# RetNet recurrence with RWKV channel mix: order of the first loads, scaling per 256 tokens, mixes in halves, one function table

## The chip, the cores and the metric

The kernel runs on one core of a Trainium2 chip. The metric is device time in microseconds (us), from launch to end. The numbers of before are the median, the lowest and the highest of three runs, and one profiled execution beside them, whose trace all the lines below come from. Its engines are TensorE (PE, with its weight loads as PEld), VectorE (DVE), ScalarE (ACT), GpSimd (POOL) and SyncE (SP).

## The reference

Two layers follow each other. The first is a retention layer: for each batch (4) and head (8) a 64x64 state decays by a factor per head and takes in k times v at each of 768 tokens; q times the state is the output. The second is a channel mix: each token is mixed with the one before it by two vectors, then goes through two products with a squared ReLU between them, and through a sigmoid gate.

```python
def _attn_ref(q, k, v):
    ...
    for t in range(S):
        state = gamma[None, :, None, None] * state + np.einsum('bhd,bhe->bhde', k[:, :, t], v[:, :, t])
        y[:, :, t] = scale * np.einsum('bhd,bhde->bhe', q[:, :, t], state)
    return y

def _moe_ref(x, mu_k, mu_r, w_k, w_v, w_r):
    x_prev = ...                      # x, one token later; zero at the first
    xk = mu_k * x + (1.0 - mu_k) * x_prev
    xr = mu_r * x + (1.0 - mu_r) * x_prev
    k = np.maximum(xk @ w_k, 0.0)
    v = k * k @ w_v
    r = 1.0 / (1.0 + np.exp(-(xr @ w_r)))
    return r * v
```

x is the first layer's output with its 8 heads side by side (512 wide); the hidden width is 1024. q, k, v, the weights and the output are float32 in memory.

## The kernel before

**Tiling.** The 4 x 768 tokens are cut into 24 chunks of 128 tokens; two chunks make a block of 256, of which there are 12 (three to a batch). The first layer works chunk by chunk. Inside a chunk the recurrence is a masked product of q and k (`scores`, `masked`) times v, and between chunks a 64x64 state for each head is carried (`state`, `kept`). The second layer works block by block.

**One chunk of the first layer.** `load_q` and `load_v` bring 256 KB each through GpSimd's DMA queue, cast to float16; `load_k` brings k as float32 through SyncE's. `scale_k` (L169) multiplies k by the decay of each token and casts it (`ks`): on VectorE in the first two blocks, on GpSimd after them. `transposes` (L177) turns q and ks on TensorE, `transposed` (L181) copies the result out on ScalarE (`qkT`). `scores` (L188) multiplies, `masked` (L196) applies the mask on VectorE (`a2t`). `state` (L208, L216) and `kept` (L225, `sbd`) carry the state. `result` (L236, L242) makes the output in PSUM, and `decayed` (L252) writes it, times a table of decay powers `gy`, into `xT`, where a batch stands with its channels on the partitions.

**One block of the second layer.** `differ` (L266) takes xT minus xT one token earlier (`dx`): on VectorE in the first two blocks, on GpSimd after them. `mixed` (L272) makes `xk` and `xr` from it, four instructions each on VectorE, each with two float32 inputs in SBUF (`dx` and `xT`). `keys` (L282) is the product with w_k in four groups, `squared` (L292, L293) does ReLU and square on ScalarE; `gate` (L298) and `opened` (L305) do the product with w_r and the sigmoid for two halves of 128 tokens; `values` (L313) is the product with w_v, two parts for each half; `store` (L322) multiplies both on VectorE and sends the result through SyncE's queue.

**What sets the order.** Nothing is scheduled by a planner at build time. Each step is put into one list by `at` with a time, the list is sorted, and the steps are emitted in that order; each engine and each DMA queue then runs its own instructions in the order of emission and waits for what they need. The times come from the table `ORDER`, in units in which a block has T = 12: `att` has the offsets of the first layer's steps for the first and second chunk of a block (`scale`, `T` and `TC` for transposing and copying, `S` and `SE` for the state, `A`, `M`, `Y`, `YE` for scores, mask, result and output), and of `dx`, `xk` and `xr`; `mix` has those of the second layer (`G` keys, `K` squares, `R` and `RS` gate, `V` values, `O` store); `load` those of the loads of q and v from chunk 6 on; `start` the places of the first four blocks. From block 4 on the first layer runs two blocks ahead of the second.

**The start.** At time -9T come the loads: k of chunks 0 and 1 on SyncE with the constants between them, then on GpSimd q and v of chunks 0 to 3, both halves of w_k, q and v of chunks 4 and 5, w_r and both halves of w_v. k has two buffers of one chunk (`ldk`), so that k of chunk c + 2 is fetched when chunk c has been scaled (L341). `constants` (L374) also makes `gy` on VectorE: a copy and seven doublings for each of the two chunk parities, 14 multiplies (L386).

Of the kernel before, what the change touches and what calls it, by code (L numbers as in the profile page):

```python
# [9 lines left out]
F16 = mybir.dt.float16  # L10
F32 = mybir.dt.float32
# [38 lines left out]
def kernel(  # L50
# [40 lines left out]
    g0_np = 0.125 * KSC * np.stack([gam[h_pj] ** -C, one], axis=1)  # L91
# [10 lines left out]
    ld = pool("ld", 8)  # L102
# [49 lines left out]
    def load_k(c):  # L152
        b, t = tok(c)
        K32[c] = ldk.tile([P, H, D], F32, name="k32")
        nc.sync.dma_start(out=K32[c], in_=k[b, :, t, :].rearrange("h t d -> t h d"))

    def load_q(c):
        b, t = tok(c)
        Q16[c] = ld.tile([P, H, D], F16, name="q16")
        nc.gpsimd.dma_start(out=Q16[c], in_=q[b, :, t, :].rearrange("h t d -> t h d"))  # L160

    def load_v(c):
        b, t = tok(c)
        V16[c] = ld.tile([P, H, D], F16, name="v16")
        nc.gpsimd.dma_start(out=V16[c], in_=v[b, :, t, :].rearrange("h t d -> t h d"))  # L165

    def scale_k(c, eng):
        KS[c] = att.tile([P, H, D], F16, name="ks16")
        eng.tensor_tensor(  # L169
            out=KS[c], in0=K32[c], in1=gk[:, c % 2, :, None].to_broadcast([P, H, D]), op=ALU.mult  # L170
        )

    def transposes(c):
        PT[c] = psa.tile([P, 2, NJ, C], F16, name="pT", tag="a")
        for i, src in enumerate((Q16[c], KS[c])):
            for j in range(NJ):
                nc.tensor.transpose(PT[c][:, i, j, :], src[:, 2 * j : 2 * j + 2, :], ident)  # L177
# [284 lines left out]
```

## Time and profile before

| | |
|---|---|
| median of three runs | 189.29 us (188.75 to 189.69) |
| the profiled execution | 187.1 us |
| its span, first to last instruction | 185.3 us |
| granted TensorE clock | 0.999 |
| busy share: PE, DVE, ACT, POOL | 85%, 81%, 51%, 48% |
| matmuls | 1416 |
| DMA packets | 82336, of which 76560 under 512 bytes |
| HBM read, written | 24.22 MB, 6.29 MB |

The span is what the instructions take; the rest of the profiled execution's time lies before the first and after the last of them. Busy shares are means over the whole span. A matmul's duration includes the time in the pipeline, so that chained matmuls overlap; the chain of waits gives the time from one to the next. In the rows, a line such as L272 is a line of the kernel; `x4` is a count; a row of the timeline has start, duration, engine, line and tile, and in brackets the idle time before it and what ended it. A row of a line's own view has least, median and longest duration in ns. The row of a DMA issue has its size at the destination and the time from issue to landing. Where busy time by stage is shown, the last three columns are the granted clock, the DMA engines' share and GB/s.

### The profile page before, as it was taken

Reading aid. Unit: us, or ns where it says so; the run is one execution under the profiler, and the core shown is the slowest. Engines: PE = TensorE matmul, PEld = TensorE weight load, DVE = VectorE, ACT = ScalarE, POOL = GpSimd, SP = SyncE. Lnnn points to the kernel's source line nnn. Section 1 sums busy time; section 2 is a strip of 40 time slices with the busy share of each in tenths; the row PEclk is TensorE's granted clock in tenths of the full one; section 3 lists DMA queues with packets and bytes.
Section 4 is the critical chain, followed back from the end, with each engine's and each line's share of the span. In section 5 each row is a group of like instructions: output and inputs, shape, how many; then the busy total and the mean of one; then the engine's idle time right before and its main releaser. Section 6 shows DMA issues by size and latency. Waiting matters only on the chain.

```text
span 185.3 us, 3522 instructions
## 1 busy us (share of the span) xinstructions
PE 156.7 (85%) x1416; PEld 101.5 (55%) x1416; DVE 149.7 (81%) x237; ACT 94.3 (51%) x146; POOL 88.1 (48%) x87
## 2 busy tenths in 40 slices
PE   0374069899699999999899899899799899999991
PEld 0253047774375675558358468467367367475740
DVE  0845599995939798899999989999999989795511
ACT  2120121999374475508808709709519529557650
POOL 7993120407995793938809709619528021040000
PEclk9999999999999999999999999999999999999999
DMA  6999999920999899797993994995984111011112
GB/s 89 166 167 192 177 178 195 179 47 0 118 187 196 192 170 135 94 144 167 130 152 74 141 128 80 142 161 56 181 125 31 58 57 60 2 57 57 60 57 113
DMA packets 82336, 21.83 MB, mean 118 GB/s; under 512 B 76560, under 2 KB 79248, under 8 KB 82320
## 3 DMA queue, kind: packets, MB, share of 16 engines
q0 software_dynamic: 52560, 8.92, 61.5%
q1 hardware_dynamic: 28704, 12.69, 28.4%
q8 instruction: 11, 0.18, 0.4%
q10 hardware_dynamic: 1056, 0.00, 0.3%
q14 instruction: 5, 0.04, 0.1%
HBM read 24.22 MB, written 6.29 MB: 165 GB/s over the span
## 4 chain that ended last, share of the span: by engine, by line
PE 45%; DVE 37%; DMA 10%; ACT 2%; POOL 2%; issue 1%; SPq 1%; DVEq 0%
PE pV L313 15%; PE pZ L282 15%; DVE xr L272 14%; DVE xk L272 12%; DMA k<-in_k_dram 10%; PE pY L242 4%; PE pR L298 4%; DVE osb L322 3%; PE pA L188 3%; DVE a2t L196 3%; PE pY L236 3%; DVE sbd L225 2%; POOL dx L266 2%; DVE xT L252 2%; ACT k L293 1%
## 5 line engine op out<-in xcount | busy, mean ns | idle before, releaser
L292 ACT ACTIVATE kr<-pZ 128x512 f32<-128x512 f32 x48 | 28.4, 592 | 47.8 <-PE pZ L282 47.8
L282 PE MATMUL pZ<-xk,wk 128*128 128x256 f16 x384 | 47.8, 274 | 2.3 <-DVE xk L272 2.3
L313 PE MATMUL pV<-wv,k 128*128 128x512 f16 x192 | 49.0, 380 | 0.2 <-DVE osb L322 0.2
L266 POOL TENSOR_TENSOR dx<-xT 128x1024 f32<-128x1024 f32 x10 | 19.2, 1918 | 60.0 <-DVE xT L252 60.0
L272 DVE SCALAR_TENSOR_TENSOR xr<-dx,mur,xT 128x256 f16<-128x256 f32 x48 | 42.5, 944 | 0.0
L282 PEld LDWEIGHTS <-wk 128*128 128x128 f16 x384 | 36.4, 98 | 9.3 <-issue 3.0
L181 ACT COPY qkT<-pT 128x1024 f16<-128x1024 f16 x24 | 24.1, 1005 | 27.2 <-PE pT L177 27.0
L196 DVE TENSOR_TENSOR a2t<-pA,c_sb 128x512 f16<-128x512 f32 x48 | 30.1, 678 | 2.5 <-PE pA L188 2.5
L272 DVE SCALAR_TENSOR_TENSOR xk<-dx,muk,xT 128x256 f16<-128x256 f32 x48 | 28.8, 657 | 2.9 <-POOL dx L266 2.8
L293 ACT ACTIVATE k<-kr 128x512 f16<-128x512 f32 x48 | 30.2, 630 | 1.6
L169 POOL TENSOR_TENSOR ks<-k,csm_sb 128x512 f16<-128x512 f32 x20 | 22.8, 1143 | 12.1 <-DVE sbd L225 7.8
L313 PEld LDWEIGHTS <-k 128*128 128x128 f16 x192 | 16.9, 98 | 17.5 <-issue 0.8
L322 DVE SCALAR_TENSOR_TENSOR osb<-pV,rsb 128x512 f32<-128x512 f32 x24 | 16.4, 682 | 10.6 <-PE pV L313 7.3
L298 PE MATMUL pR<-wr,xr 128*128 128x512 f16 x96 | 24.1, 380 | 0.0
L160 POOL DMA_DIRECT2D q<-in_q_dram x24 | 22.2, 924 | 0.8 <-POOLq L446 0.8
L165 POOL DMA_DIRECT2D v<-in_v_dram x24 | 21.9, 914 | 0.0
L252 DVE TENSOR_TENSOR xT<-pY,gy_sb 128x512 f32<-128x512 f32 x24 | 16.5, 688 | 3.0 <-PE pY L242 2.8
L305 ACT ACTIVATE rsb<-pR 128x512 f32<-128x512 f32 x24 | 14.1, 590 | 6.5 <-PE pR L298 6.5
L177 PE MATMUL pT<-c_sb,q 128*128 128x128 f16 x96 | 10.2, 234 | 7.6 <-DMA q<-in_q_dram 7.6
L225 DVE TENSOR_TENSOR sbd<-pS,csm_sb 128x512 f16<-128x512 f32 x20 | 13.6, 681 | 3.1 <-PE pS L216 3.1
L298 PEld LDWEIGHTS <-xr 128*128 128x128 f16 x96 | 8.7, 98 | 10.0 <-DVE xr L272 0.6
L177 PEld LDWEIGHTS <-q 128*128 128x128 f16 x96 | 7.5, 104 | 10.3 <-DMA q<-in_q_dram 7.9
(26 smaller groups left out, 101.9 us busy)
## 6 DMA issues: line engine op xcount, KB each, us to landing
k<-in_k_dram SPq DMA_DIRECT2D x24, 256.0 KB, 5.4
out_dram<-osb SPq DMA_DIRECT2D x24, 256.0 KB, 2.3
q<-in_q_dram POOLq DMA_DIRECT2D x24, 128.0 KB, 4.8
v<-in_v_dram POOLq DMA_DIRECT2D x24, 128.0 KB, 5.8
wk<-in_moe_w_k_dram POOLq DMA_DIRECT2D x2, 512.0 KB, 12.1
wv<-in_moe_w_v_dram POOLq DMA_DIRECT2D x2, 512.0 KB, 18.5
wr<-in_moe_w_r_dram POOLq DMA_DIRECT2D x1, 512.0 KB, 17.5
c_sb<-c SPq DMA_DIRECT2D x1, 64.0 KB, 3.6
```

Source lines behind the costliest of these rows:

```text
L160: nc.gpsimd.dma_start(out=Q16[c], in_=q[b, :, t, :].rearrange("h t d -> t h d"))
L169: eng.tensor_tensor(out=KS[c], in0=K32[c], in1=gk[:, c % 2, :, None].to_broadcast([P, H, D]), op=ALU.mult)
L181: nc.scalar.copy(out=QKT[c], in_=PT.pop(c))
L196: nc.vector.tensor_tensor(out=A2[c][:, hp], in0=PA[c][hp], in1=causal[:, None, :].to_broadcast([P, NJ, C]), op=ALU.mult,)
L266: eng.tensor_tensor(out=DX[m], in0=xcur, in1=xprev, op=ALU.subtract)
L272: nc.vector.scalar_tensor_tensor(out=dst[m][:, j], in0=DX[m][:, j], scalar=mu[:, j : j + 1], in1=xprev[:, j], op0=ALU.mult, op1=ALU.add,)
L282: nc.tensor.matmul(pZ[:, i, :], lhsT=wk16[:, co, fo * P : fo * P + P], rhs=XK[m][:, co, :], start=(i == 0 and co == 0), stop=(co == NCO - ...
L292: nc.scalar.activation(out=kr, in_=PZ.pop((m, g)), func=AF.Relu)
L293: nc.scalar.activation(out=K2[m][:, 2 * g : 2 * g + 2], in_=kr, func=AF.Square)
L298: nc.tensor.matmul(pR, lhsT=XR[m][:, co, tb * P : tb * P + P], rhs=wr16[:, co, :], start=(co == 0), stop=(co == NCO - 1),)
L313: nc.tensor.matmul(PV[m, tb], lhsT=K2[m][:, fo, tb * P : tb * P + P], rhs=wv16[:, fo, :], start=(fo == 0), stop=(fo == NFO - 1),)
L322: nc.vector.scalar_tensor_tensor(out=osb, in0=PV.pop((m, tb)), scalar=1.0 / (KSC * KSC), in1=RS.pop((m, tb)), op0=ALU.mult, op1=ALU.mult,)
```

## The change

Six things, all in the order and the size of steps; what is computed stays the same.

1. **First loads.** k of chunks 0 to 3 is fetched through GpSimd's queue, and the queue's order becomes q, k, v of chunk 0, then of chunk 1, 2 and 3, then w_k as before. From chunk 4 on k stays on SyncE.
2. **Loads per 256 tokens.** The tiles of q, k and v hold a block. Each is filled by two DMAs of the same size as before, issued one after the other. k has two buffers of a block; the fetch of block n + 2 follows the scaling of block n. From block 3 on q and v have a place of their own in the order (`load`).
3. **Scaling per 256 tokens.** On GpSimd one instruction scales a block. In the first two blocks VectorE still scales chunk by chunk (`first`).
4. **Mixes in halves.** `mixed` does two of its four instructions at a time, each half with an offset of its own.
5. **Decay powers.** Only the even parity is built by doublings (`powers`); the odd one is one multiply from it (`powers2`). Both have a place of their own in the order.
6. **Function table.** A sigmoid of one column is run in `constants`, ahead of all other work of ScalarE.

All offsets of `ORDER` are new. The diff, cut where lines only follow from these:

```diff
     "att": {
-        "scale": (-5.73, -4.03),
-        "T": (0.1, 2.32),
-        "TC": (2.23, 4.28),
-        "S": (1.83, 6.57),
-        "SE": (2.9, 11.39),
-        "A": (2.81, 7.79),
-        "M": (6.42, 8.52),
-        "Y": (8.93, 10.34),
-        "YE": (9.06, 10.4),
-        "dx": (13.61,),
-        "xk": (14.87,),
-        "xr": (24.22,),
+        "scale": (-7.68,),
+        "first": (-5.03, 0.72),
+        "T": (-0.46, 2.67),
+        "TC": (-0.22, 2.89),
+        "S": (2.03, 6.44),
+        "SE": (5.18, 12.2),
+        "A": (2.77, 6.47),
+        "M": (5.73, 6.77),
+        "Y": (9.29, 9.58),
+        "YE": (9.85, 10.67),
+        "dx": (13.42,),
+        "xk": (16.2, 19.85),
+        "xr": (20.59, 24.83),
     },
     "mix": {
-        "G": (-0.77, -0.76, 0.13, 1.84),
-        "K": (1.66, 2.09, 2.54, 6.09),
-        "R": (4.78, 5.13),
-        "RS": (6.11, 6.32),
-        "V": (5.05, 8.3, 9.91, 11.44),
-        "O": (10.22, 13.1),
+        "G": (-0.23, 1.28, 1.46, 3.99),
+        "K": (1.25, 2.04, 5.34, 7.41),
+        "R": (5.52, 6.1),
+        "RS": (8.35, 7.64),
+        "V": (7.19, 9.1, 5.17, 11.79),
+        "O": (11.75, 12.54),
     },
-    "load": (7.46, 14.36, 10.71, 5.01),
+    "load": (2.6, 7.43),
+    "pw": (-82.96, -75.01),
     "start": {
-        0: (-7.04, -3.15, -2.4, -0.25),
-        1: (-6.26, -2.28, -0.66, 0.5),
-        2: (-2.89, 0.5, 1.71, 3.0),
-        3: (0.54, 2.3, 2.54, 2.28),
+        0: (-6.32, -3.29, -2.16, -0.56),
+        1: (-5.68, -2.52, -1.23, 0.33),
+        2: (-2.79, 0.09, 1.24, 1.03),
+        3: (0.28, 2.72, 1.95, 2.85),
     },
...
-    ld = pool("ld", 8)
+    ld = pool("ld", 5)
...
+    def load(n, c, x, eng, tiles, name, dt):
+
+        if n not in tiles:
+            tiles[n] = (ldk if dt is F32 else ld).tile([P, 2, H, D], dt, name=name)
+        for i in range(2) if c is None else (c,):
+            eng.dma_start(out=tiles[n][:, i], in_=rows(x, n)[:, i])
+
+    def load_k(n, c=None):
+        load(n, c, k, nc.sync if c is None else nc.gpsimd, K32, "k32", F32)
...
+    def scale_k(n, c, eng):
+        if n not in KS:
+            KS[n] = att.tile([P, 2, H, D], F16, name="ks16")
+        e = slice(0, 2) if c is None else slice(c, c + 1)
+        w = gk[:, e, :, None].to_broadcast([P, e.stop - e.start, H, D])
+        eng.tensor_tensor(out=KS[n][:, e], in0=K32[n][:, e], in1=w, op=ALU.mult)
...
-    def mixed(m, dst, mu, name):
+    def mixed(m, dst, mu, name, half):
...
-        for j in range(NJ):
+        for j in range(2 * half, 2 * half + 2):
             nc.vector.scalar_tensor_tensor(
...
     def attention(n, t0, w=1.0):
         start = n < 2
+        o = lambda name, i=0: t0 + w * EV[name][i]
+        if not start:
+            at(o("scale"), scale_k, n, None, nc.gpsimd)
+        if n + LDK < NBLK:
+            at((max(o("first", 0), o("first", 1)) if start else o("scale")) + 0.01, load_k, n + LDK)
...
+        warm = const.tile([P, 1], F32, name="warm")
+        nc.vector.memset(warm, 0.0)
+        nc.scalar.activation(out=warm, in_=warm, func=AF.Sigmoid)
...
+    def powers2():
+        needs(("gy", 0))
+        done.add(("gy", 1))
+        nc.vector.tensor_tensor(
+            out=gy[:, 1], in0=gy[:, 0], in1=g0[:, 1, :, None].to_broadcast([P, NJ, C]),
+            op=ALU.mult,
+        )
...
-    at(t, load_k, 0)
     at(t, constants)
-    at(t, load_k, 1)
-    for c in range(4):
-        at(t, load_q, c)
-        at(t, load_v, c)
+    for n in range(2):
+        for c in range(2):
+            at(t, load_q, n, c)
+            at(t, load_k, n, c)
+            at(t, load_v, n, c)
     at(t, load_wk, 0)
     at(t, load_wk, 1)
...
+    for n in range(3, NBLK):
+        at((n - 4) * T + LQ[0], load_q, n)
+        at((n - 4) * T + LQ[1], load_v, n)
+    at(ORDER["pw"][0], powers)
+    at(ORDER["pw"][1], powers2)
```

More of the change, by code (lines that the diff above doesn't have):

```diff
@@ new lines, in load_k, with load_q, load_v @@
+    def load_k(n, c=None):
+        load(n, c, k, nc.sync if c is None else nc.gpsimd, K32, "k32", F32)
+    def load_q(n, c=None):
+        load(n, c, q, nc.gpsimd, Q16, "q16", F16)
+    def load_v(n, c=None):
+        load(n, c, v, nc.gpsimd, V16, "v16", F16)
+    def scale_k(n, c, eng):
[4 more added lines that the diff above has]
+        eng.tensor_tensor(out=KS[n][:, e], in0=K32[n][:, e], in1=w, op=ALU.mult)
+        done.update(("ks", 2 * n + i) for i in range(e.start, e.stop))
@@ L173, in transposes, with heads @@
+    def heads(tiles, c, a, n):
+        return tiles[c // 2][:, c % 2, a : a + n, :]
     def transposes(c):
         PT[c] = psa.tile([P, 2, NJ, C], F16, name="pT", tag="a")
-        for i, src in enumerate((Q16[c], KS[c])):
+        needs(("ks", c))
+        for i, src in enumerate((Q16, KS)):
             for j in range(NJ):
-                nc.tensor.transpose(PT[c][:, i, j, :], src[:, 2 * j : 2 * j + 2, :], ident)
+                nc.tensor.transpose(PT[c][:, i, j, :], heads(src, c, 2 * j, 2), ident)
@@ L202, in state @@
     def state(c):
+        needs(("ks", c))
         first = c % NCH == 0
@@ L248, in decayed @@
     def decayed(c):
+        needs(("gy", c % 2))
         done.add(("x", c))
@@ L266, in differ @@
         eng.tensor_tensor(out=DX[m], in0=xcur, in1=xprev, op=ALU.subtract)
[L268 removed]
+    def mixed(m, dst, mu, name, half):
         xprev = shifted(m)[1]
[L270 to L271 removed]
+        if m not in dst:
+            dst[m] = mix.tile([P, NJ, TM], F16, name=name)
+        done.add((name, m, half))
+        for j in range(2 * half, 2 * half + 2):
             nc.vector.scalar_tensor_tensor(
@@ L330 @@
     T = 12.0
+    LDK = 2
     EV = ORDER["att"]
```

80 lines of the change are left out of this document (30 added, 50 removed).

## The prediction

> **What bounds the kernel now.** I read the page first (span, DMA by slice), then busy time by stage, then the steady stage period by period, then the chain and the timelines of VectorE and GpSimd.
>
> ```profile
> span 185.3 us, 3522 instructions
> ```
> ```profile
> DMA  6999999920999899797993994995984111011112
> ```
>
> ```profile
> 30.40:45.50 15.10, 14.53 (x141) 10.59 (x142) 12.80 (x24) 13.07 (x21) 4.44 (x3) 1.00 0.55 96
> 45.50:84.20 38.70, 36.17 (x339) 22.68 (x337) 32.82 (x50) 18.90 (x30) 28.41 (x29) 1.00 1.36 153
> 84.20:151.60 67.40, 62.86 (x591) 40.49 (x589) 65.97 (x89) 37.86 (x60) 35.48 (x32) 1.00 0.82 110
> 151.60:181.30 29.70, 29.70 (x227) 18.48 (x224) 19.71 (x34) 19.13 (x32) 3.89 (x2) 1.00 0.14 53
> ```
>
> The columns after the stretch are PE, PEld, DVE, ACT and POOL busy. The DMA engines are full for the first 37 us; from 84 to 151 VectorE is busy 65.97 of 67.40 us; from 151.6 TensorE is busy without a gap. So there are three limits in turn: arrival of data, VectorE, TensorE.
>
> The start, from the chain of waits:
>
> ```profile
> 8.62 12.11 DMA k<-in_k_dram
> ...
> 23.81 2.46 DVE xk L272 x4
> ...
> 30.38 1.43 PE pZ L282 x8
> ```
>
> Chunk 3 of k is issued at 8.62 and lands at 20.73. VectorE stands in its queue before that chunk's scaling, with the outputs of block 0 behind it, so the first key matmul starts only at 30.38.
>
> The steady stage: five periods, cut at the starts of the differences on GpSimd (84.23, 97.66, 111.38, 124.52, 137.97, 151.65). First all instructions summed, then the mixes (L272) alone, then one period of POOL and the mixes beside it, then four mixes late in the run with POOL idle:
>
> ```profile
> sum 67.42, PE 62.88 PEld 40.52 DVE 65.98 ACT 37.83 POOL 35.48; mean PE 12.58 PEld 8.10 DVE 13.20 ACT 7.57 POOL 7.10
> ```
> ```profile
> sum 67.42, DVE 37.02; mean DVE 7.40
> ```
> ```profile
> 97.66 1.88 POOL L266 TENSOR_TENSOR dx<-xT 128x1024 f32<-128x1024 f32 x1 [5.56 <-DVE xT L252]
> 99.50 0.91 POOL L160 DMA_DIRECT2D q<-in_q_dram  x1
> 100.41 0.88 POOL L165 DMA_DIRECT2D v<-in_v_dram  x1
> 101.30 1.06 POOL L169 TENSOR_TENSOR ks<-k,csm_sb 128x512 f16<-128x512 f32 x1
> ```
> ```profile
> L272 DVE SCALAR_TENSOR_TENSOR xr<-dx,mur,xT x1: 1810/1810/1810, 98.0 to 98.0; 128x256 f16<-128x256 f32 x1
> ```
> ```profile
> L272 DVE SCALAR_TENSOR_TENSOR xr<-dx,mur,xT x1: 1259/1259/1259, 99.8 to 99.8; 128x256 f16<-128x256 f32 x1
> ```
> ```profile
> 167.47 1.66 DVE L272 SCALAR_TENSOR_TENSOR xk<-dx,muk,xT 128x256 f16<-128x256 f32 x4
> ```
>
> A free mix takes 1.66/4 = 0.415 us of VectorE (0.40 from start to start when chained), eight 3.2 us. A period spends 7.40 on them: 4.2 us of stall. The mix at 98.02 ends at 99.83, 0.29 after the difference ends at 99.54; the one that starts at 99.8 takes 1.26, 0.8 too much, while POOL issues q and v. So VectorE without stalls needs 13.20 - 4.2 = 9.0 us a period, and the period is 67.42/5 = 13.48.
>
> What TensorE needs, from a stretch of the chain in which it runs without a gap:
>
> ```profile
> 153.49 0.45 PE pT L177 x8
> 153.93 0.87 PE pZ L282 x8
> 154.81 0.22 PE pS L208
> 155.02 0.22 PE pS L216 x4
> ...
> 157.87 0.86 PE pV L313 x4
> ...
> 159.59 0.33 PE pA L188 x8
> ...
> 160.89 0.22 PE pY L236 x4
> 161.12 0.34 PE pY L242 x8
> ```
>
> A block is four pZ groups (3.48), four pV and two pR of the same width (6 x 0.86 = 5.16), and twice pT, pA, pS and both pY (2 x 1.56 = 3.12) with one state copy (0.22): 12.0 us. That is the floor of a period.
>
> **The change part by part.**
>
> *Order of the first loads.* Each load moves 256 KB out of HBM:
>
> ```profile
> q<-in_q_dram POOLq DMA_DIRECT2D x1, 128.0 KB, 5.9
> ```
> ```profile
> k<-in_k_dram SPq DMA_DIRECT2D x1, 256.0 KB, 7.0
> v<-in_v_dram POOLq DMA_DIRECT2D x1, 128.0 KB, 8.3
> ```
> ```profile
> 1.26 1.06 POOL L160 DMA_DIRECT2D q<-in_q_dram  x1 [0.82 <-POOLq L446]
> ```
> ```profile
> 7.52 0.93 POOL L165 DMA_DIRECT2D v<-in_v_dram  x1
> ```
>
> The first q lands at 1.26 + 5.9 = 7.2, the fourth v at 7.52 + 8.3 = 15.8. In between land v0 to v3, q1 to q3, and k1 and k2 (7.9 and 14.9): nine loads in 8.6 us, 0.96 each. After the change k3 is the eleventh load of GpSimd's queue and q0, k0, v0 are the first three. Taking the third at 7.2 as now (k0 lands earlier still, and k1 just after it), k3 lands at 7.2 + 8 x 0.96 = 14.9, and at 15.8 if one of chunks 4 and 5, which SyncE now fetches as soon as chunks 0 and 1 are scaled, slips in between. I take 15.8. The other end: the eight loads of GpSimd alone came 8.6/7 = 1.23 apart, which gives 7.2 + 10 x 1.23 = 19.5. Issues at 0.9 us each end at about 12, so they stay ahead. The four extra issues put wk's issue 3.5 us later, but the bytes ahead of it are the same ones, so it lands about as now.
>
> From k3 to the first key matmul it is now 30.4 - 20.7 = 9.7 us. The new order takes the second output xT of block 0 (0.6) ahead of k3's scaling, and the stall in the four mixes at 23.81 is gone (2.46 - 1.66 = 0.8), as the first scaling on POOL now stands behind four more issues: 9.7 - 0.6 - 0.8 = 8.2, rounded. So the first pZ comes at 24.0 (15.8 + 8.2), **-6.4**; ends 14.9 + 8.2 = 23.1 (-7.3) and 19.5 + 9.7 = 29.2 (-1.2).
>
> Speaking against this step: the Trainium skill, "DMA: Bandwidth & Descriptors", section "Issuing engine by pattern", puts plain loads on SyncE and calls that path generally faster. By it k would be slower from GpSimd; here the gain comes from order, not from the path, and a microsecond more in landing would make this term -5.4.
>
> *Decay factors and function table.*
>
> ```profile
> 4.98 2.28 DVE L386 TENSOR_TENSOR gy_sb<-gy_sb,csm_sb 128x4 f32<-128x4 f32 x14
> ```
> ```profile
> 41.83 1.28 ACT L305 ACT_TABLE_LOAD   x1
> ```
>
> Seven of fourteen multiplies go (half of 2.28, 1.1 us), and one of 128x512 comes, an estimated 0.7 (the 128x512 operation of L322, shown below, takes 682 ns), at a point where VectorE waits for k anyway. The first scaling waits for k0 now, so I take 0 (-1.1 to +0.7). The second table load sits in the stretch where ScalarE is busy 13.07 of 15.10 us and the first keys wait for its squares: **-0.7**, the middle of 0 and -1.3. Without that queue it would be nothing.
>
> *Scaling per 256 tokens.* Two scalings of 1.06 become one of about 2.1. POOL is busy 7.10 of 13.48, so its own time costs nothing. Load counts stay the same: two issues per tensor and block, both now in a row. The scaling waits for both chunks of k; these are fetched when the scaling two blocks earlier frees the buffer, some 24 us ahead. If that cover were gone, the q and v issues and the next difference would queue behind it on POOL. Cost 0, but the scaling holds a mix it meets for up to 2.1 us instead of 1.06.
>
> *Mixes in halves.* In the new order the steady cycle of VectorE after the last output xT is: output O, state SE, O, half of xr, half of xk, SE, four masks, half of xk, half of xr, two xT. POOL after that xT: difference, two q issues, scaling, two v issues. The three operations beside the difference are of the kind that doesn't stall:
>
> ```profile
> L322 DVE SCALAR_TENSOR_TENSOR osb<-pV,rsb 128x512 f32<-128x512 f32 x24 | 16.4, 682 | 10.6 <-PE pV L313 7.3
> ```
>
> 682 ns on the mean, with its 24 spread over the whole run. So the difference (1.4 us of stall) meets no mix. The first mixes come 2 us after xT, just as the difference ends, and run into the q issues and the scaling: I count one mix held by an issue (0.8) and one by the scaling (2.1 at most). The second four come after 2.4 us of masks, when POOL's last issues are over (2.0 + 0.9 + 0.9 + 2.1 + 0.9 + 0.9 = 7.7 after xT; these mixes start at about 9). Stalls 2.9, plus some 0.5 of waiting for TensorE as now (13.48 - 13.20 = 0.3, and a little more): 9.0 + 2.9 + 0.5 = 12.4, above the floor of 12.0. Five periods: 5 x (13.48 - 12.4) = **-5.4**; ends -7.4 (at 12.0) and 0 (the stalls move to other mixes), and a loss in the rival below.
>
> *The rest.* 45.5 to 84.2: TensorE is busy 36.17 of 38.70, so at most -2.5; its order there is new, which may open gaps of the same size. 0. From 151.6 on TensorE is full with the same matmuls: 0.
>
> Sum: -6.4 - 0.7 - 5.4 = -12.5. The profiled execution took 187.1 us (span 185.3 and 1.8 around it): 174.6. The median of the runs, 189.29, stands 2.2 above the profiled one; with the same distance **176.8 us**.
>
> **The rivals.**
>
> *Only the tensor operations of GpSimd stall a mix.* Then q and v issues cost nothing, the first four mixes fit between difference and scaling, VectorE needs under 12, and TensorE's floor of 12.0 decides: -7.4 for the period term, 174.8 us. Against it: the 1.26 us mix at 99.8, which no difference or scaling overlaps. This is what the Trainium skill, "SBUF — State Buffer", section "Who interferes with whom", says: a VectorE instruction with two SBUF inputs contends with a GpSimd instruction that reads SBUF, not with one that only writes. The trace agrees for the difference (0.29 us after its end) and not for the issues. Chance 0.12.
>
> *The loads are the limit at the start whatever their order.* For it: the DMA row is full for eight slices, and bytes stay the same; if GpSimd's queue takes k at 1.23 us a load, only -1.2 is left there: -7.3 in all, 182.0 us. Against it: k2 and k3 waited while wk, needed later, was served. Chance 0.13.
>
> *The stalls only move.* POOL has 7.1 us of work a period and VectorE 13; if as many mixes meet it as now, the period stays 13.48 and -7.1 remains: 182.2 us. Chance 0.13.
>
> *Slower: the longer scaling and the paired issues catch the mixes.* After the difference POOL runs four issues and a doubled scaling without a break. If the difference holds one mix (1.4), four issues one each (0.8) and the scaling one (1.9), that is 6.5 a period: 15.5, +2.0 x 5 = +10.1, less 7.1: +3.0, 192.3 us. It decides from 4.2 + 7.1/5 = 5.6 us of stall a period. For it: now five of eight mixes stall in a period. Against it: the order puts masks and state products, which don't stall, over half of POOL's chain. Chance 0.12.
>
> *It doesn't do what it says.* The offsets only set the order on each engine; if waits elsewhere line the engines up as now, and chunk 3 isn't what holds the start, nothing changes: 189.3 us. Chance 0.08.
>
> **How the numbers follow.** My own case has 0.42 and by itself 172 to 181. Faster by over 0.5% (about 0.9 us, what a measurement here can tell from none): 0.42 + 0.12 + 0.13 + 0.13 = 0.80; within 0.5%: 0.08; slower: 0.12. The range of 168 to 186 takes in the two partial cases at 182 and the gains at their far ends (-7.3 - 1.3 - 7.4 - 2.5 = -18.5, which is 170.8; 168 leaves 2.8 more, since all terms come from one execution); it leaves out the last two cases.
>
> **What would show it.** k3's landing near 16 and the first pZ near 24; one table load only; differences on GpSimd 12.0 to 12.8 us apart in the steady stage and the mixes at about 6 us a period instead of 7.40; TensorE still without a gap over its last 30 us. It is wrong if the first pZ stays near 30, if the mixes keep 7 us or more a period, or if TensorE now waits in the stretch from 40 to 80 for weights or for the second block's scaling.

## The result and the profile after

The changed kernel takes 177.76 us (median of four runs, 177.45 to 178.88), where the kernel before took 189.02 (188.23 to 189.69) beside it: a ratio of 0.942, with a 95% interval of 0.936 to 0.948. The profiled execution took 177.48 us. In three of the kernels below (mixes_in_fours, scale_before_dx, idle_by_chunk) the profiled execution is one of the longer ones, so that of these only spots and stretches are read and not the whole span.

The span of after, from its page of the profile:

```profile
span 175.7 us, 3484 instructions
```

The span is 9.6 us shorter (185.3 to 175.7). Busy time by stage, cut at the same four instructions in both kernels: the first difference on GpSimd (block 2), that of block 5, that of block 10, the end. First after, then before; the columns are PE, PEld, DVE, ACT and POOL busy, then the granted clock, the DMA share and GB/s.

```profile
0.00:36.75 36.75, 24.75 (x255) 17.94 (x256) 28.64 (x59) 16.40 (x24) 20.10 (x27) 1.00 1.41 173
36.75:79.88 43.13, 40.77 (x368) 25.27 (x367) 37.53 (x53) 21.22 (x33) 31.09 (x27) 1.00 1.39 162
79.88:142.36 62.48, 60.56 (x580) 39.24 (x579) 60.94 (x88) 37.38 (x59) 33.16 (x26) 1.00 0.77 102
142.36:175.70 33.34, 29.38 (x220) 18.14 (x217) 17.67 (x34) 18.68 (x32) 3.79 (x2) 1.00 0.17 64
```
```profile
0.00:42.98 42.98, 25.40 (x255) 18.66 (x256) 29.92 (x64) 16.23 (x22) 17.80 (x24) 1.00 1.27 150
42.98:84.23 41.25, 38.72 (x351) 23.87 (x350) 33.45 (x51) 21.10 (x34) 30.93 (x31) 1.00 1.28 143
84.23:151.65 67.42, 62.88 (x591) 40.52 (x589) 65.98 (x89) 37.83 (x60) 35.48 (x33) 1.00 0.82 110
151.65:185.30 33.65, 29.66 (x226) 18.43 (x224) 20.35 (x35) 19.13 (x32) 3.89 (x2) 0.99 0.16 61
```

By stage that is -6.2, +1.9, -4.9 and -0.3. The +1.9 is not a loss. In the second stage TensorE now does 368 matmuls instead of 351 and is busy 40.77 instead of 38.72 us; its idle time there is 2.4 us, as before (2.5). The difference of block 5 simply stands later in TensorE's order now, and the later two stages have that work less to do (580 and 220 against 591 and 226). The first differences stand at the same place, with 255 matmuls ahead of them in both kernels. So the account that holds is: 6.2 us up to the first difference, and 3.4 after it (142.3 to 138.9). Of the 3.4, 2.8 is idle time of TensorE (11.1 to 8.2 us, worked out from the rows above), and most of that lies in the third stage (4.5 to 1.9).

The start, from the chain of waits and TensorE's timeline of after:

```profile
10.16 6.79 DMA k<-in_k_dram
```
```profile
23.73 0.39 PE L299 MATMUL pZ<-xk,wk 128*128 128x256 f16 x2
```

Chunk 3 of k lands at 16.95 instead of 20.73, and the first key matmul starts at 23.7 instead of 30.3.

One steady period of after, GpSimd and then VectorE, and the mixes (L288) alone over the five periods of the third stage:

```profile
92.45 1.89 POOL L280 TENSOR_TENSOR dx<-xT 128x1024 f32<-128x1024 f32 x1 [5.26 <-DVE xT L266]
94.30 1.80 POOL L163 DMA_DIRECT2D q<-in_q_dram  x2
96.10 1.93 POOL L179 TENSOR_TENSOR ks<-k,csm_sb 128x1024 f16<-128x1024 f32 x1
97.95 1.82 POOL L163 DMA_DIRECT2D v<-in_v_dram  x2
```
```profile
94.02 4.30 DVE L288 SCALAR_TENSOR_TENSOR xr<-dx,mur,xT 128x256 f16<-128x256 f32 x2
98.24 0.87 DVE L288 SCALAR_TENSOR_TENSOR xk<-dx,muk,xT 128x256 f16<-128x256 f32 x2
```
```profile
L288 DVE SCALAR_TENSOR_TENSOR xr<-dx,mur,xT x2: 605/2186/3768, 94.0 to 94.5; 128x256 f16<-128x256 f32 x2
```
```profile
sum 62.48, DVE 33.33; mean DVE 6.67
```

The difference hardly meets a mix now: the first one starts shortly before its end and takes 0.605 us instead of 0.47. (In the first of the five periods it still holds one, for 1.80 us in all at 80.25.) The second mix takes 3.77 us: it starts at 94.5, beside the q issues, and is let go only at 98.3, 0.29 us after the scaling has ended at 98.03. The two mixes beside the v issues (98.24) are free, as are the second four. The mixes take 6.67 us a period instead of 7.40, and four of the five periods are 12.57 or 12.58 us long and the last 12.17; the mean is 12.50 instead of 13.48.

### The profile page after: what moved, and what is told of

Its sections match the earlier page's. It is cut to its first block, busy times and chain, and to the rows that moved or that the text cites. A ratio compares the mean times of both kernels' runs of the same rounds, so it can differ in the third digit from the quotient of the medians.

```text
span 175.7 us, 3484 instructions
## 1 busy us (share of the span) xinstructions
PE 155.5 (88%) x1416; PEld 100.6 (57%) x1416; DVE 144.8 (82%) x232; ACT 93.7 (53%) x146; POOL 88.1 (50%) x81
## 4 chain that ended last, share of the span: by engine, by line
PE 41%; DVE 34%; POOL 14%; issue 4%; DMA 4%; POOLq 0%
PE pV L331 14%; PE pZ L299 11%; DVE xr L288 11%; DVE xk L288 8%; PE pR L316 6%; POOL q L163 5%; DVE a2t L209 5%; DMA k<-in_k_dram 4%; POOL v L163 3%; DVE xT L266 3%; POOL dx L280 3%; DVE osb L340 3%; DVE sbd L238 3%; PE pY L255 3%; PE pT L190 2%
## 5 line engine op out<-in xcount | busy, mean ns | idle before, releaser
L331 PE MATMUL pV<-wv,k 128*128 128x512 f16 x192 | 47.1, 380 | 0.0
L288 DVE SCALAR_TENSOR_TENSOR xr<-dx,mur,xT 128x256 f16<-128x256 f32 x48 | 41.1, 898 | 0.0
L309 ACT ACTIVATE kr<-pZ 128x512 f32<-128x512 f32 x48 | 28.4, 592 | 15.8 <-PE pZ L299 15.8
L288 DVE SCALAR_TENSOR_TENSOR xk<-dx,muk,xT 128x256 f16<-128x256 f32 x48 | 27.5, 619 | 3.7 <-POOL dx L280 3.7
L331 PEld LDWEIGHTS <-k 128*128 128x128 f16 x192 | 17.7, 98 | 17.2
L316 PE MATMUL pR<-wr,xr 128*128 128x512 f16 x96 | 23.2, 380 | 2.4 <-DVE xr L288 2.4
L323 ACT ACTIVATE rsb<-pR 128x512 f32<-128x512 f32 x24 | 13.0, 594 | 16.8 <-PE pR L316 16.8
L179 POOL TENSOR_TENSOR ks<-k,csm_sb 128x1024 f16<-128x1024 f32 x10 | 19.5, 1953 | 0.1
L266 DVE TENSOR_TENSOR xT<-pY,gy_sb 128x512 f32<-128x512 f32 x24 | 15.7, 680 | 0.4 <-PE pY L255 0.3
L190 PE MATMUL pT<-c_sb,ks 128*128 128x128 f16 x96 | 10.2, 234 | 3.1 <-DVE ks L179 3.1
```

The costliest lines, as they stand in the source:

```text
L190: nc.tensor.transpose(PT[c][:, i, j, :], heads(src, c, 2 * j, 2), ident)
L288: nc.vector.scalar_tensor_tensor(out=dst[m][:, j], in0=DX[m][:, j], scalar=mu[:, j : j + 1], in1=xprev[:, j], op0=ALU.mult, op1=ALU.add,)
L309: nc.scalar.activation(out=kr, in_=PZ.pop((m, g)), func=AF.Relu)
L316: nc.tensor.matmul(pR, lhsT=XR[m][:, co, tb * P : tb * P + P], rhs=wr16[:, co, :], start=(co == 0), stop=(co == NCO - 1),)
L331: nc.tensor.matmul(PV[m, tb], lhsT=K2[m][:, fo, tb * P : tb * P + P], rhs=wv16[:, fo, :], start=(fo == 0), stop=(fo == NFO - 1),)
```

## The experiments

For each kernel: median, ratio to the kernel before on its chip, start of the first key matmul, start of the first difference on GpSimd, and the time from there to the end of the span (these three from its profiled execution). The kernel before had medians of 189.02, 187.03, 188.43 and 186.85 us on the four chips, and the kernel after had ratios of 0.942 and 0.956 on two of them. Ratios from different chips that lie within 0.015 are therefore not told apart here.

| kernel | median us | ratio (95%) | first pZ | first dx | dx to end |
|---|---|---|---|---|---|
| before | 189.02 | 1 | 30.3 | 42.98 | 142.3 |
| after | 177.76 | 0.942 (0.936 to 0.948) | 23.7 | 36.75 | 138.9 |
| k_on_sync_late | 189.54 | 1.016 (1.009 to 1.023) | 28.7 | 48.56 | 139.5 |
| k_on_sync_early | 180.13 | 0.966 (0.958 to 0.974) | 24.1 | 38.85 | 139.3 |
| mixes_in_fours | 185.28 | 0.986 (0.974 to 0.998) | 25.0 | 38.39 | 145.8 |
| mixes_in_idle | 173.18 | 0.928 (0.920 to 0.936) | 23.1 | 36.51 | 134.3 |
| two_tables | 179.51 | 0.962 (0.956 to 0.968) | 24.0 | 38.86 | 139.0 |
| scale_by_chunk | 174.39 | 0.933 (0.925 to 0.941) | 24.7 | 38.10 | 134.4 |
| scale_before_dx | 179.94 | 0.955 (0.945 to 0.966) | 23.5 | 38.22 | 140.9 |
| after_again | 178.71 | 0.956 (0.949 to 0.964) | 24.8 | 38.35 | 138.9 |
| two_tables_again | 179.78 | 0.964 (0.958 to 0.971) | 24.0 | 38.84 | 138.9 |
| idle_by_chunk | 174.60 | 0.934 (0.925 to 0.943) | 23.6 | 40.83 | 134.1 |
| fill_gap | 178.02 | 0.956 (0.949 to 0.964) | 23.4 | 37.36 | 139.0 |

The last column falls into few values: what a kernel does to the start is seen in the first difference, and what it does to the steady stage in the rest.

### Does chunk 3 of k hold the start?

k_on_sync_late sends k of chunks 0 to 3 through SyncE again, with one buffer of a block, so that chunks 2 and 3 wait for the scaling of 0 and 1:

```diff
-    ldk = pool("ldk", 2)
+    ldk = pool("ldk", 1)
...
-        load(n, c, k, nc.sync if c is None else nc.gpsimd, K32, "k32", F32)
+        load(n, c, k, nc.sync, K32, "k32", F32)
...
-    LDK = 2
+    LDK = 1
...
+    at(t, load_k, 0, 0)
     at(t, constants)
+    at(t, load_k, 0, 1)
     for n in range(2):
         for c in range(2):
             at(t, load_q, n, c)
-            at(t, load_k, n, c)
             at(t, load_v, n, c)
```

> The changed kernel with k of chunks 0 to 3 back on SyncE and one buffer of a block instead of two, so that k of chunks 2 and 3 is fetched only when chunks 0 and 1 are scaled, as before the change. Theory (chunk 3 of k holds the start): it lands near 20 instead of 16.95, the first pZ comes at 26 to 28 instead of 23.7, the time goes up by 2 to 4 us to 180 to 182. Rival (the loads are the limit whatever their order): first pZ within 0.5 us of 23.7 and the time within 0.5% of 177.8.

Its chain of waits, and its first products on TensorE:

```profile
8.66 13.36 DMA k<-in_k_dram
...
23.18 13.30 DMA k<-in_k_dram
```
```profile
28.72 3.80 PE L299 MATMUL pZ<-xk,wk 128*128 128x256 f16 x32
...
38.64 0.61 PE L190 MATMUL pT<-c_sb,ks 128*128 128x128 f16 x4 [5.89 <-POOL ks L179]
```

Chunk 3 lands at 22.02, 5.1 later than in after, and the first key matmul starts 5.0 later: one to one, as the first step of the prediction has it. The whole kernel loses 12 us, not 5, because the same single buffer also holds chunks 4 and 5, of which the second lands at 36.48. TensorE waits 5.89 us for block 2 and then runs at a granted clock of 0.50 from 38.5 to 42. From the first difference on nothing is lost (139.5).

k_on_sync_early keeps two buffers of a block and issues all four on SyncE at the start, so that q and v have GpSimd's queue to themselves:

```diff
-        load(n, c, k, nc.sync if c is None else nc.gpsimd, K32, "k32", F32)
+        load(n, c, k, nc.sync, K32, "k32", F32)
...
+    at(t, load_k, 0, 0)
     at(t, constants)
+    at(t, load_k, 0, 1)
+    at(t, load_k, 1, 0)
+    at(t, load_k, 1, 1)
     for n in range(2):
         for c in range(2):
             at(t, load_q, n, c)
-            at(t, load_k, n, c)
             at(t, load_v, n, c)
```

> The changed kernel with k of chunks 0 to 3 on SyncE, all four issued at once, two block buffers kept; q and v in GpSimd's queue in the old order. Theory (what counts is that k is issued ahead of w_k and not behind a buffer): k3 lands by 17, the time stays within 1% of 177.8. Rival (GpSimd's queue itself is what counts, since SyncE's packets are served less often beside it): k3 at 19 or later, first pZ at 26 or later, 180 us or more.

From its chain of waits and TensorE's timeline:

```profile
3.19 7.30 DMA q<-in_q_dram
```
```profile
24.07 0.61 PE L299 MATMUL pZ<-xk,wk 128*128 128x256 f16 x2
```

Here chunk 3 of k lands at 13.1, 3.8 earlier than in after, and the first key matmul starts at 24.1 all the same (23.7 and 24.8 in the two profiles of after): what is late now is q of chunk 1, which lands at 10.49. So k is the thing that holds the start only while it is the last to come. GpSimd's queue itself brings nothing that these runs show; what counts is that the four chunks are asked for early. The time is not within the 1% that was expected: the ratio of 0.966 lies above both of after (0.942 and 0.956), but by only 0.010 above the nearer, so that no difference is shown.

### Where the mixes stand

mixes_in_fours puts the mixes of blocks 2 to 11 back into two groups of four:

```diff
-            at(o("xk", i), mixed, n, XK, muk, "xk16", i)
-            at(o("xr", i), mixed, n, XR, mur, "xr16", i)
+            if start:
+                at(o("xk", i), mixed, n, XK, muk, "xk16", i)
+                at(o("xr", i), mixed, n, XR, mur, "xr16", i)
+            else:
+                at(t0 + 14.87 + 0.001 * i, mixed, n, XK, muk, "xk16", i)
+                at(t0 + 24.22 + 0.001 * i, mixed, n, XR, mur, "xr16", i)
```

> The changed kernel with the mixes of blocks 2 to 11 four in a row again, at the offsets of before (xk 14.87, xr 24.22); all else as changed. Theory (the mixes that meet GpSimd's operations set the period): differences on GpSimd 13.2 to 13.8 us apart in the steady stage instead of 12.5, 182 to 186 us. Rival (the order chain between TensorE and VectorE sets it): period within 0.2 of 12.5, time within 1% of 177.8.

mixes_in_idle is the same edit with 19.84 and 20.59, after the masks, where GpSimd has nothing to do:

> The changed kernel with all eight mixes of a block (blocks 2 to 11) placed together after the masks, where GpSimd has finished its chain; all else as changed. Theory (stalls beside GpSimd set the period): no mix over 1 us in the steady stage, period at TensorE's 12.0 to 12.2, time 171 to 175 us. Rival (order chain): mixes free, but period still 12.4 to 12.6 and time within 1% of 177.8, VectorE idle instead.

The mixes alone, over four periods of the first and five of the second, and the steady stage of the second:

```profile
sum 57.89, DVE 30.52; mean DVE 7.63
```
```profile
sum 60.11, DVE 16.25; mean DVE 3.25
```
```profile
79.14:139.25 60.11, 60.01 (x578) 39.19 (x576) 45.15 (x88) 37.86 (x59) 32.99 (x27) 1.00 0.80 106
```

In fours the mixes take 7.63 us a period. Its first three periods are 13.60, 14.43 and 13.83 us long at a granted clock of 1.00; the fourth is 16.03, at 0.89. So the place of the mixes sets the period. Not all of this loss is held mixes: over the five periods VectorE is idle for 6.1 of 70.66 us (1.5 of 62.48 in after), so the place also makes the engines wait for each other. In the idle time all eight take 3.25 us, which is eight free mixes. VectorE is then busy 45.15 of 60.11 us and TensorE 60.01, so TensorE's own work is the floor; four of the five periods are 12.23 or 12.43 us long. The rest of the kernel after the first difference takes 134.3 us instead of 138.9. So the place of the mixes still cost the change 4.6 us.

### What the doubled scaling costs

scale_by_chunk keeps everything of the change, but scales a block in two instructions, one behind the other:

```diff
-            at(o("scale"), scale_k, n, None, nc.gpsimd)
+            at(o("scale"), scale_k, n, 0, nc.gpsimd)
+            at(o("scale"), scale_k, n, 1, nc.gpsimd)
```

> The changed kernel with GpSimd's scaling as two instructions of 128x512, one behind the other, instead of one of 128x1024. Theory (each GpSimd instruction holds the mix that it meets, and a mix gets in between two): the longest mix of the steady stage falls from 3.77 to about 2.7 us, the next one is held too, period 12.2 to 12.6, time within 1% of 177.8. Rival (the double length is what costs): the sum of the mixes falls by 1 us a period and the time by 3 us or more.

GpSimd and VectorE in one of its periods, and the mixes alone in it:

```profile
106.36 2.26 POOL L179 TENSOR_TENSOR ks<-k,csm_sb 128x512 f16<-128x512 f32 x2
```
```profile
104.47 1.66 DVE L288 SCALAR_TENSOR_TENSOR xr<-dx,mur,xT 128x256 f16<-128x256 f32 x2
106.05 2.85 DVE L288 SCALAR_TENSOR_TENSOR xk<-dx,muk,xT 128x256 f16<-128x256 f32 x2
```
```profile
102.71:114.94 12.23, 6.10 (x8) 1.00 1.00 130
```

I had expected no gain, since the next mix would be held instead. More mixes are indeed held (27 over 0.6 us in the whole run instead of 16), but none takes more than 1.81 us, and the sum of a period falls to 6.10. That is enough for TensorE to become the bound: 12.23 from one difference to the next, 134.4 us from the first one to the end, as with the mixes in the idle time. Of the 4.5 us gained, 2.8 come between the differences of blocks 2 and 5 (40.31 instead of 43.13, with TensorE idle for 0.3 instead of 2.4) and 1.5 in the five periods after them. So the part "scaling per 256 tokens" costs this kernel 4.5 us by itself, and the change is faster in spite of it.

scale_before_dx moves the doubled scaling ahead of the difference (its offset from -7.68 to -10.7), so that behind the difference come only the issues of q and v:

> The changed kernel with GpSimd's scaling put ahead of the difference, so that the first four mixes of a period meet only the q and v issues. Theory of the prediction (issues hold a mix too): one or two mixes of 1.2 to 2 us remain there, period 12.0 to 12.4. Rival (only GpSimd's operations that read SBUF hold a mix): all mixes beside the issues take 0.47 us; period 12.0 if nothing else holds.

GpSimd, VectorE and the mixes (L288) in one of its steady periods, then its steady stage:

```profile
109.11 1.89 POOL L280 TENSOR_TENSOR dx<-xT 128x1024 f32<-128x1024 f32 x1 [4.85 <-DVE xT L266]
110.95 1.83 POOL L163 DMA_DIRECT2D q<-in_q_dram  x2
112.76 1.78 POOL L163 DMA_DIRECT2D v<-in_v_dram  x2
```
```profile
110.88 0.87 DVE L288 SCALAR_TENSOR_TENSOR xr<-dx,mur,xT 128x256 f16<-128x256 f32 x2
111.67 2.52 DVE L288 SCALAR_TENSOR_TENSOR xk<-dx,muk,xT 128x256 f16<-128x256 f32 x2
```
```profile
L288 DVE SCALAR_TENSOR_TENSOR xk<-dx,muk,xT x4: 474/478/2126, 106.1 to 113.7; 128x256 f16<-128x256 f32 x4
```
```profile
86.00:145.80 59.80, 59.60 (x580) 39.26 (x579) 52.77 (x88) 37.40 (x59) 31.26 (x25) 1.00 0.80 106
```

A mix that starts at 111.7 takes 2.13 us while GpSimd's rows show nothing but the issues of q and v, although the two mixes before it run free beside the first q issue. The scaling follows the issues at 114.51. That looks as if issues held a mix too, but other places speak against it. First, the mixes beside the same four issues (q, q, v, v) of the first block on GpSimd, in after and in scale_by_chunk; then VectorE and GpSimd in k_on_sync_late:

```profile
L288 DVE SCALAR_TENSOR_TENSOR xk<-dx,muk,xT x1: 2123/2123/2123, 39.1 to 39.1; 128x256 f16<-128x256 f32 x1
```
```profile
L288 DVE SCALAR_TENSOR_TENSOR xk<-dx,muk,xT x1: 1259/1259/1259, 41.6 to 41.6; 128x256 f16<-128x256 f32 x1
```
```profile
66.94 1.68 DVE L288 SCALAR_TENSOR_TENSOR xk<-dx,muk,xT 128x256 f16<-128x256 f32 x4 [0.51 <-POOL dx L280]
68.53 0.88 DVE L288 SCALAR_TENSOR_TENSOR xr<-dx,mur,xT 128x256 f16<-128x256 f32 x2
```
```profile
71.96 1.90 POOL L179 TENSOR_TENSOR ks<-k,csm_sb 128x1024 f16<-128x1024 f32 x1 [1.53 <-DMA k<-in_k_dram]
```

The issues are alike in after and scale_by_chunk, but the held mix takes 2.12 us in the one and 1.26 in the other (where a second one is held as long, one for each of the two scalings behind the issues). These are the times of a mix that starts inside the scaling itself, of 128x1024 (2.12 at 42.31 in after) and of 128x512 (1.26 at 44.81 in scale_by_chunk). In k_on_sync_late six mixes run free beside four issues (66.86 to 70.43), while the scaling behind them still waits for its k. And in none of the thirteen profiles is a mix held beside issues that have the difference as GpSimd's next operation. So the hold beside issues goes with a scaling that stands ready behind them. That it is this scaling, at work before its row begins, is inferred from these times; no row shows it. The Trainium skill, "SBUF — State Buffer", section "Who interferes with whom", lets only GpSimd instructions that read SBUF contend with a VectorE instruction of two SBUF inputs. The six free mixes beside issues agree with that.

In the steady stage TensorE is full (59.60 of 59.80). In blocks 2 to 4, where GpSimd's operations follow each other for 14 us (from 38.22) and 11 us (from 55.78) on end, the moved scaling holds mixes for up to 3.56 us, TensorE waits for them, and its granted clock falls to 0.82 between 55.78 and 74.98. The time as a whole is as in after.

### What the second function table costs

two_tables takes the early sigmoid out, so that the table is loaded in the middle again:

```diff
-        warm = const.tile([P, 1], F32, name="warm")
-        nc.vector.memset(warm, 0.0)
-        nc.scalar.activation(out=warm, in_=warm, func=AF.Sigmoid)
```

> The changed kernel without the early sigmoid, so that ScalarE loads its table a second time at the first gate. Prediction's term: 0.7 us slower (0 to 1.3). Rival (ScalarE has slack there): no difference that can be told, under 0.3 us.

It came out some 2 us behind after, but on another chip, and its first difference was late before the table was loaded. So the same kernel was run again beside after on one chip:

> The kernel after without the early sigmoid, so that ScalarE loads its second function table at about 39. Theory (the prediction's -0.7): this load lies in the stretch in which the squares of the first blocks hold TensorE, and costs 0.7 to 1.3 us beside the kernel after on the same chip. Rival: ScalarE has slack there and the difference seen earlier (about 2 us, from other chips) was TensorE's slow first product: then both start the third difference at the same time to 0.5 us whenever their first products run at the same rate, and the times differ by less than 0.5.

> The kernel after, unchanged, as the measure for the other three. Expected: ratio to before 0.935 to 0.95, steady period 12.57. Open is the first product with w_k: in the first profile of this kernel its 32 matmuls followed each other at 0.11 us; if TensorE's slow rate at the start ends at a moment that shifts from run to run, they may take 0.16 here, and the third difference then starts up to 2 us later than 36.75; if the moment is fixed by this program's own timing, it starts at 36.5 to 37.

TensorE's timeline of two_tables_again with ScalarE's load, then TensorE's of after_again with ScalarE's first sigmoids, then the second sigmoid of before:

```profile
37.96 3.63 PE L316 MATMUL pR<-wr,xr 128*128 128x512 f16 x16
41.42 0.81 PE L331 MATMUL pV<-wv,k 128*128 128x512 f16 x3
```
```profile
38.97 1.28 ACT L323 ACT_TABLE_LOAD   x1
```
```profile
37.47 3.63 PE L316 MATMUL pR<-wr,xr 128*128 128x512 f16 x16
40.93 1.24 PE L331 MATMUL pV<-wv,k 128*128 128x512 f16 x5
```
```profile
39.41 1.09 ACT L323 ACTIVATE rsb<-pR 128x512 f32<-128x512 f32 x2 [0.94 <-PE pR L316]
```
```profile
44.03 0.60 ACT L305 ACTIVATE rsb<-pR 128x512 f32<-128x512 f32 x1 [0.27 <-PE pR L298]
```

Gate products and the first values are 3.46 us apart in both kernels. The load takes 1.28 us, but ScalarE stands idle for 0.94 us at this point without it, and TensorE does not wait for the rest. What separates the two (0.49 us) is there before the load begins and stays the same until the first difference (38.84 against 38.35). In before the load ended at 43.11, the first sigmoid followed at once, and the second already waited 0.27 us for TensorE, so nothing was lost there either. So the load costs nothing in these traces, as the rival has it. The times alone do not decide: the medians, 179.78 (178.91 to 181.00) and 178.71 (178.22 to 181.02), are 1.07 us apart and their ranges overlap.

### A better version, and TensorE's half rate at the start

idle_by_chunk joins the edits of mixes_in_idle and scale_by_chunk:

> The kernel after with both edits that made it faster: the scaling as two instructions of 128x512, and all eight mixes of blocks 2 to 11 where GpSimd has nothing to do. Theory (both edits take away the same held mixes, and TensorE's 12.0 to 12.2 us a period is then the floor): it is as fast as the better of the two alone, ratio to before 0.918 to 0.930, period 12.1 to 12.3. Rival (the gains add, as the mixes left are held in other ways): 3.4 us below the mixes in the idle time alone, ratio about 0.908.

Its runs (173.35 to 176.75 us) lie below all of after_again on the same chip (178.22 to 181.02). From the first difference on it takes 134.1 us, about as each edit does alone (134.3 and 134.4): the gains don't add, as TensorE is the floor. Which of the three is best is not told apart. In its profile the first difference is late (40.83), and two stretches of TensorE say why, by timeline and by window:

```profile
32.02 0.38 PE L230 MATMUL pS<-v,ks 128*128 128x128 f16 x4 [2.78 <-DMA v<-in_v_dram]
...
33.71 3.75 PE L299 MATMUL pZ<-xk,wk 128*128 128x256 f16 x24
```
```profile
30.00:32.00 2.00, 0.00 (x0) 0.00 (x0) 2.00 (x6) 1.58 (x3) 0.00 (x0) 1.00 1.26 192
32.00:34.00 2.00, 1.98 (x22) 1.52 (x22) 1.67 (x5) 0.72 (x1) 0.00 (x0) 0.57 1.25 193
```

TensorE waits 2.78 us for a v, and then the granted clock is 0.57. The same 24 matmuls take 2.85 us in after (30.53), at a granted clock of 1.00.

At the start there is such a slow stretch in every kernel. fill_gap puts ten matmuls that nobody reads where TensorE otherwise waits for k of chunk 2:

```diff
+    def filler():
+        pf = psm.tile([P, 2 * P], F32, name="pF", tag="m")
+        for i in range(10):
+            nc.tensor.matmul(pf, lhsT=ident, rhs=c16, start=(i == 0), stop=(i == 9))
...
+                if c == 2:
+                    at(o("S", i) - 0.0001, filler)
                 at(o("S", i), state, c)
```

> The kernel after with ten matmuls of 128x128 by 128x256 that nobody reads, put ahead of the state product of chunk 2, where TensorE otherwise stands idle for some 2 us (16.2 to 18.3) while k of chunk 2 is on its way. Theory (TensorE runs at half rate until it has been busy without a gap for a few us): the fast rate comes at 17 to 20 instead of 22.6, groups of four transposes of chunk 2 take 0.39 instead of 0.6, and the first product runs at 0.11 us a matmul in every profile; the end moves by less than 1 us against the kernel after if that had a fast first product already, and by up to -2 if not. Rival (the rate does not depend on what TensorE did): the groups still take 0.6 until 22 or later, and the ten matmuls only push back what follows.

The first product with w_k in after and in after_again (the same program), a group of transposes in after_again, and the filler with the same group in fill_gap:

```profile
24.44 3.72 PE L299 MATMUL pZ<-xk,wk 128*128 128x256 f16 x30 [0.32 <-DVE xk L288]
```
```profile
19.58 0.63 PE L190 MATMUL pT<-c_sb,q 128*128 128x128 f16 x4
...
24.75 5.46 PE L299 MATMUL pZ<-xk,wk 128*128 128x256 f16 x32
```
```profile
16.15 1.93 PE L382 MATMUL pF<-c_sb 128*128 128x256 f16 x10
...
18.62 0.39 PE L190 MATMUL pT<-c_sb,q 128*128 128x128 f16 x4
```

In after the matmuls of this product follow each other at 0.11 us. In after_again they do so at 0.21 until the middle of the product, and at 0.11 from there. With the gap filled, the fast rate is there at 18.2, when the filler ends, and the first product runs at 0.11 throughout. A product that is fast from the start proves little, as after has one too. But in none of the eleven other profiles of the changed kernel and its variants does the fast rate come before 21.6. So the theory is borne out, by one profile: the rate follows what TensorE has been doing. The first difference comes 1.0 us earlier than in after_again (37.36 against 38.35), though not than in after (36.75); the medians (178.02 and 178.71) don't tell the two apart.

## Why the prediction was right, step by step

**The start, -6.4: right in sum, from two misses.** The first key matmul starts at 23.7 (24.0 was predicted) and 6.6 us earlier than before. But k of chunk 3 lands at 16.95 instead of 15.8, and from there to the matmul it takes 6.8 us instead of 8.2. The landing lies between the two ends that the step gave: the eight loads behind v of chunk 0 (landed at 7.51) came 1.18 us apart instead of 0.96. The way behind it is shorter by 1.4 us because of the mixes of block 0. Before, all four (2.46 at 23.81) stand between chunk 3's scaling and the second `kept`, for which TensorE waits; after, that `kept` runs first (19.40) and the mixes follow it (20.01). So the whole 2.46 leaves the way and not only the 0.8 of stall that the step took out. That k holds the start is shown by k_on_sync_late, 5.0 for 5.1 us. k_on_sync_early, where k comes through the other queue and the first key matmul starts at 24.1, speaks for the early request and not for the queue. How much the start gains also hangs on when TensorE's fast rate comes: in after_again, where it comes later, chunk 3 lands at 17.38, the first key matmul starts at 24.75 and the first difference at 38.35, 1.6 us later than in after.

**The function table, -0.7: wrong.** It took half of the load's duration because the load stands in a busy stretch. The traces of the kernel with and without it show 0: ScalarE waits for the gate product there anyway, in before as well. A busy share of 13.07 in 15.10 over a stretch says nothing on the one spot.

**The decay powers, 0: right.** The first scaling on VectorE waits for k of chunk 0 (2.35 us in after), not for the multiplies.

**The scaling per 256 tokens, "cost 0, but it holds a mix": the mechanism was right, the cost was not 0.** Undoing this one part gains 4.5 us behind the first difference. The next term has the stall in the steady stage; the 2.8 us between the differences of blocks 2 and 5 stand in no term.

**The steady stage, -5.4: mechanism right, size too large.** The difference hardly meets a mix and the second four are free, as the step said. Of the first four one is held by 3.3 us, through the q issues and the doubled scaling in one piece; I had counted two mixes, held by 0.8 and 2.1. The 0.8 was put down to an issue. What the runs show in its place is a hold that goes with the scaling behind the issues and depends on its width: 0.8 us for 128x512, 1.65 for 128x1024. Mixes were to take about 6 us a period; over the five periods they take 6.67. The period is 12.50 on the mean instead of 12.4, and the term -4.9. Some 2 us of that is work which TensorE now does before the difference of block 5, so its real worth is nearer 3: the differences on GpSimd were taken as marks of progress, and they stand at another place in TensorE's order now.

**Blocks 2 to 4, 0: right** by TensorE's idle time (2.4 against 2.5 us), although by the differences it looks like a loss of 1.9. But scale_by_chunk shows that these 2.4 us were not bound to stay: without the doubled scaling they are 0.3. **The tail, 0: right** (-0.3).

**The sum.** In the profiled executions the gain is 9.6 us, against 12.5 predicted: up to the first difference 6.2 against 7.1 (the table's 0.7 is most of what is missing), and behind it 3.4 against 5.4. In after_again, the same program on another chip, it is 8.1 (185.3 to 177.2). The median came out within 1 us of the prediction because the kernel before has a median 1.9 us above its own profiled execution and the kernel after only 0.3; carrying the 2.2 us over brought the prediction closer by chance. The loads per 256 tokens, the decay powers and the other new offsets were not run alone, so what each of them adds stays open.

**The rivals.** "Only the tensor operations of GpSimd stall a mix" is what the free mixes of k_on_sync_late point to, against my case. Its time does not follow from it, as the doubled scaling holds a mix beside the issues as well; the first four mixes do not fit in between. "The loads are the limit whatever their order" falls with chunk 3's landing, though k_on_sync_early shows that q takes its place when k comes 3.8 us earlier still. "The stalls only move" was half true: 0.7 of 7.40 us a period went away. The slower case did not come: in a steady period the q issues and the doubled scaling hold one mix, and the mixes beside the v issues are free.

## What to carry to other kernels

Where GpSimd's operations hold VectorE's two-input operations, count what one held operation can meet in one piece; two short GpSimd operations let it through between them, and placing the mixes where GpSimd rests removes the cost altogether. A mix beside load issues is not safe when such an operation stands ready behind them. Cut stages at points that stand at the same place in the bounding engine's own order (count its instructions on both sides), or moved work will look like a gain in one stage and a loss in the next. Whether a piece of work on a busy engine costs anything is read at its own spot, from what the engines beside it wait for in that microsecond, and not from busy shares over a stretch.

## What the runs showed of the hardware that was not expected

TensorE's rate at the start differs between executions of one program: 128x256 matmuls 0.11 us apart from the first product on in one profile of the kernel after, 0.21 up to the middle of this product in the other. The granted clock is 1.00 in these rows at both rates; only after a wait does it show the half rate. It is 0.57 after 2.78 us of idle time in idle_by_chunk. In scale_before_dx, whose matmuls run at the fast rate from 21.9 on, it is 0.50 from 26 to 28, after a wait of 0.92 us; fill_gap keeps the fast rate through a wait of 1.24 us (25.02), so that the length of one wait does not decide it. The Trainium skill, "TensorE: Matmul & The Clock Gate", section "Part 1: The HAM clock gate (the "warmup" mystery)", says that the array runs at half clock until it has been busy for one activity window of about 3.4 us, and that the window runs freely, so the moment shifts from run to run. The two rates and the shift agree with that; the waits of 2.78 and 0.92 us that brought the half rate back are shorter than the idle window of about 3.4 us that it names.

And a GpSimd operation does not only delay a mix by what is left of it: the mix that started beside the q issues was not let in between the issue and the scaling behind it, and came free 0.29 us after the second had ended. Between two scalings of 128x512 it was: one mix ends 0.29 us after the first of them (107.72 in scale_by_chunk), and the next is held by the second.
